# Batch 0 of a fused attention and MLP kernel: eleven idle matmuls ahead of k^T v, and v copied beside a column of ones

## The chip, the cores and the metric

The kernel runs on one core of one Trainium2 chip. The metric is the device time of one execution, in microseconds (us). Four executions of the kernel before gave 299.22, 299.75, 300.38 and 301.85 us, with a median of 300.06 us. The profile is that of one of them, the execution that took 299.22 us.

## The reference

Two stages follow each other. The first is a linear attention with cosine weights, for 8 batches, 8 heads, 576 positions and 64 columns a head:

```python
def phi(x, c, s):
    r = np.maximum(x, 0.0)
    return np.concatenate([r * c, r * s], axis=-1)
q_p = phi(q, cos_w, sin_w)          # 128 features a head
k_p = phi(k, cos_w, sin_w)
kv = np.einsum('bhsf,bhsd->bhfd', k_p, v)
z = np.sum(k_p, axis=2)
num = np.einsum('bhsf,bhfd->bhsd', q_p, kv)
den = np.einsum('bhsf,bhf->bhs', q_p, z)[..., None] + 1e-06
return (num / den).astype(np.float32)
```

The second is an MLP over the 4608 rows of 512 columns that come out: `h = x @ w_in` (512 by 2048), `g = h * sigmoid(1.702 h)`, `out = g @ w_out` (2048 by 512). The inputs and the output are float32.

## The kernel before

The order of instructions on each engine is written out by hand (a manual schedule); the tile framework adds the waits. The rows of x are cut into 9 blocks of 512. For each block, 16 tiles of `mm1` (L281, then gelu at L286) and four tiles of `mm2` (L321) run on TensorE, and the attention of the next batch is laid between them in pieces. Four PSUM banks serve in turn as `mm` tiles, and two pairs of banks as `at` tiles.

Nothing can cover the attention of batch 0: it is the start of the program, and the first MLP block needs it. Its order is written out ahead of the block loop. All its parts work on four heads (n = 0 or 1) or on two of four row chunks (p = 0 or 1).

- `warmup(12)` (L75): twelve matmuls on a zeroed tile, then two more ahead of each but the first transposing step.
- `prep_q0` and `turn_q0` (L364, L365): relu and cosine weights on q, transposes on TensorE, and copies to `qT` on ScalarE. Each of the four `turn_q0` takes one `mm` bank.
- `prep(0, "k", ...)` (L207 on VectorE, L205 on ScalarE): the features `kp` of k. There are 24 operations of 96 partitions by 4 heads by 64 columns: 18 of them on VectorE, and 6 (the sine weights of chunks 3 to 5) on ScalarE.
- `kv0` (L373, L375): k^T v of heads 0 to 3 in one `mm` bank, then of heads 4 and 5 and, after `num0(0, 0)`, of heads 6 and 7 in another. Each head takes six matmuls that accumulate over chunks of 96 rows. z is needed too, so each moving operand is a pattern over two 64-column pieces of the `v` tile: the piece of this head and chunk, and a piece at the tile's end that holds ones. 65 of the 128 columns that come out are copied to `kvs` by ScalarE.
- `num0` (L382): the numerator with the denominator as 65th column, for two row chunks and four heads.
- `den0` and `product0` (L394, L400, L401): on VectorE, the denominator plus 1e-6, its reciprocal, and the product, which gives `xb`.
- `turn_x0` (L409, L411): transposes of `xb` on TensorE into the rest of the numerator's own bank, and ScalarE's copy to `xT`.
- `mm1_first` (L417): `mm1` for the first four tiles of block 0, in column pieces as `xT` becomes available.

The `vt` tile, 66 columns for each chunk and head with ones in column 64 (L163), is used by the batches after the first: `prep_v_wide` (L210) copies batch 1's v there in one operation, `prep_v` (L213) those of the others, and `kv_half` (L244) multiplies with 65 columns.

GpSimd issues the loads in a fixed order (k and v of batch 0 in pieces, then w_in, w_out and the next batches); SP issues q of batch 0 and later the transposing DMAs.

Of the kernel before, what the change touches and what calls it, by code (L numbers as in the profile page):

```python
# [10 lines left out]
BF16 = mybir.dt.bfloat16  # L11
# [10 lines left out]
def kernel(  # L22
# [9 lines left out]
    nc = tc.nc  # L32
    B, H, S, D = q.shape
# [11 lines left out]
    two = ctx.enter_context(tc.tile_pool(name="two", bufs=2))  # L45
# [8 lines left out]
    def rows(c):  # L54
        return 128 if c < 4 else 64

    def wide(b, n):
        return b < 2 and n != "q"

    def krows(b, c):  # L60
        return 96 if b < 2 else rows(c)

    warm = const.tile([128, TB], BF16)
    nc.vector.memset(warm, 0.0)

    def mm_tile():
        return ps.tile([128, TB], F32, name="mm", bufs=4)

    def at_tile():
        return ps.tile([128, 2, 512], F32, name="at", bufs=2)  # L70

    def warmup(n):
        wps = at_tile()
        for _ in range(n):
            nc.tensor.matmul(wps[:, 0], warm[:, 0:128], warm, start=True, stop=True)  # L75


    state = {b: {} for b in range(B)}
    SRC = {"q": q, "k": k, "v": v}

    def load_main(b, n, h0=0, h1=H, on=nc.gpsimd):
        t = 6 if wide(b, n) else 4
        np_ = 96 if wide(b, n) else 128
        if h0 == 0:
            state[b][n] = two.tile([128, 2048 if n == "q" else 49 * D], BF16, name=n)
        on.dma_start(out=state[b][n][:np_, t * D * h0:t * D * h1].rearrange("p (h e) -> p h e", h=h1 - h0),  # L86
                     in_=SRC[n][b, h0:h1, 0:np_ * t, :].rearrange("h (p c) d -> p h (c d)", c=t))

# [9 lines left out]
    def load_all(b):  # L98
        for n in "qkv":
            load_main(b, n)  # L100
            load_tail(b, n)
# [21 lines left out]
    nc.gpsimd.iota(pos_i[:, 4:5], pattern=[[1, 1]], base=512, channel_multiplier=1)  # L123
    nc.gpsimd.iota(pos6_i, pattern=[[1, 6]], base=0, channel_multiplier=6)
    load_main(0, "k", 0, 4)
    nc.gpsimd.iota(id_i, pattern=[[1, 128]], base=0, channel_multiplier=-1)
    load_main(0, "k", 4, 8)
    load_main(0, "v", 0, 4)
    load_main(0, "v", 4, 6)
# [28 lines left out]
    kp = one.tile([128, 6, H, 2 * D], BF16, name="kp")  # L158
    vt = one.tile([128, 6, H, VW], BF16, name="vt")
    qT = one.tile([128, H, NC * 128], BF16, name="qT")  # L160
    qT_tail = one.tile([128, H, 128], BF16, name="qT_tail")
    nc.vector.memset(state[0]["v"][:, 48 * D:49 * D], 1.0)
    nc.vector.memset(vt[:, :, :, D:D + 1], 1.0)  # L163
    nc.vector.memset(qT[:, :, S:NC * 128], 0.0)
    nc.vector.memset(qT_tail[:, :, 64:128], 0.0)
# [16 lines left out]
    def part(b, n, c, h0, h1):  # L182
        if wide(b, n):
            return state[b][n][:96, 0:48 * D].rearrange("p (h c d) -> p c h d", c=6, d=D)[:, c, h0:h1]
        if c == 4:
            return state[b][n, 4].rearrange("p (h d) -> p h d", d=D)[:, h0:h1]
        return state[b][n][:, 0:32 * D].rearrange("p (h c d) -> p c h d", c=4, d=D)[:, c, h0:h1]
# [7 lines left out]
    def qn_slot(b, c):  # L195

        return state[b]["qn4"] if b < 2 and c == 4 else state[b]["qn"][:rows(c), c]

    def prep(b, n, c, h0=0, h1=H, on=(nc.vector, nc.vector)):
        r = rows(c) if n == "q" else krows(b, c)  # L200
        for cs, w in enumerate((cos6, sin6) if wide(b, n) else (cosw, sinw)):
            o = qn_slot(b, c) if n == "q" else kp[:r, c]
            oc, i, wc = o[:, h0:h1, cs * D:cs * D + D], part(b, n, c, h0, h1), w[:r, c:c + 1]
            if on[cs] is nc.scalar:
                nc.scalar.activation(oc, i, AF.Relu, scale=wc)  # L205
            else:
                nc.vector.tensor_scalar(oc, i, 0.0, wc, op0=MAX, op1=MUL)  # L207
# [149 lines left out]
    s0 = state[0]  # L357
# [7 lines left out]
        copy(qT[:, 4 * n:4 * n + 4, ds(256 * p, 256)].rearrange("p h (s t) -> p h s t", s=2), t)  # L365

    def kv0(kv, h0, h1):

        v3 = s0["v"][:96].rearrange("p (j d) -> p j d", d=D)
        for h in range(h0, h1):  # L370
            for c in range(6):
                j = h * 6 + c
                nc.tensor.matmul(kv[:, ts(h % 4, 128)].rearrange("p (j d) -> p j d", j=2), kp[:96, c, h, :],  # L373
                                 v3[:, j:49:48 - j, :], start=(c == 0), stop=(c == 5))
        nc.scalar.copy(s0["kvs"][:, h0 // 4, h0 % 4:h0 % 4 + h1 - h0, 0:D + 1],  # L375
                       kv.rearrange("p (h e) -> p h e", e=128)[:, h0 % 4:h0 % 4 + h1 - h0, 0:D + 1])

    def num0(n, p):
        nm = at_tile()
# [40 lines left out]
    AC, VE = nc.scalar, nc.vector  # L420
    kvs_new(0)
    warmup(12)

    def prep_q0(n, p, on=(VE, VE)):
# [5 lines left out]
    for n, p in ((0, 0), (0, 1), (1, 0), (1, 1)):  # L430
        if n:
            prep_q0(n, p)
        turn_q0(n, p, AC.copy)
        if (n, p) != (1, 1):
            warmup(2)
    for n in range(2):
        for c in range(6):
            prep(0, "k", c, 4 * n, 4 * n + 4, on=(VE, AC if c > 2 else VE))
    kv_lo, kv_hi = mm_tile(), mm_tile()
    kv0(kv_lo, 0, 4)  # L440
    kv0(kv_hi, 4, 6)
    na0 = num0(0, 0)
    kv0(kv_hi, 6, 8)
    product0(na0, den0(na0), 0, 0)
    nb0 = num0(1, 0)
# [30 lines left out]
    for i in range(NBLK):  # L476
        work = {n: [] for n in range(32)}
        b = i + 1
# [85 lines left out]
```

## Time and profile before

| what | value |
|---|---|
| median of four runs | 300.06 us (299.22 to 301.85) |
| profiled execution | 299.22 us |
| its span, first to last instruction | 297.3 us |
| mean granted TensorE clock | 0.994 |
| TensorE busy | 284.4 us (96%) |
| VectorE busy | 106.4 us (36%) |
| ScalarE busy | 125.8 us (42%) |
| GpSimd busy | 95.2 us (32%) |
| k^T v of batch 0 (L373) | 48 matmuls, 219 ns each from start to end, 11.5 to 15.4 us |
| idle matmuls (L75) | 18, the last ones at 8.9 us |
| first block's first full `mm1` tile (L281) | starts at 25.3 us |

In the rows of the profile, PE is TensorE's matmul, PEld its weight load, DVE is VectorE, ACT ScalarE, POOL GpSimd and SP SyncE. A row gives the start and the duration in us, the engine, the line, the operation, output and input tiles, their shapes, and how many instructions of that kind are merged in it; in brackets stand the idle time of the engine ahead of it and what ended it. A matmul's duration is that from its start to its end; in a run of them the starts lie closer together than that, so a row of several says how many were issued in how long. The granted clock is the share of full speed that the throttle left to TensorE.

### The profile page before, as it was taken

The numbers are of one execution on the slowest core, as the hardware profiler recorded it, in microseconds if no ns is written. First come the engines' busy times: TensorE is split into PE (matmuls) and PEld (weight loads), VectorE is DVE, ScalarE is ACT, GpSimd is POOL, SyncE is SP. The second block draws the span as 40 slices with busy tenths as digits, with TensorE's granted clock in tenths as the row PEclk, the third lists the DMA queues.
The fourth block names the chain that finished last, engine by engine and source line by source line (L and its number), as shares of the span: only waits on it lengthen the run. The fifth ranks groups of instructions, "written<-read, shape, count | busy, mean of one in ns | idle before, by whom it ended". The sixth has DMA issues, their size and how long they took to land.

```text
span 297.3 us, 5089 instructions
## 1 busy us (share of the span) xinstructions
PE 284.4 (96%) x1940; PEld 147.2 (50%) x1974; DVE 106.4 (36%) x357; ACT 125.8 (42%) x215; POOL 95.2 (32%) x117
## 2 busy tenths in 40 slices
PE   8778999999899999999999999999999999999994
PEld 3565456545444554455445544554455444444443
DVE  5851454683480158114811482148214200000000
ACT  6836623663126512651165116511751167127411
POOL 8532340540259015800590159004501200120021
PEclk9979999999999999999999999999999999999999
DMA  7999999599999977995799879964902510011033
GB/s 185 189 204 199 202 199 192 164 117 173 145 215 178 180 118 138 183 191 100 138 184 180 117 134 193 188 107 111 198 4 60 120 43 1 35 71 37 0 70 71
DMA packets 87303, 39.65 MB, mean 133 GB/s; under 512 B 57136, under 2 KB 85040, under 8 KB 87280
## 3 DMA queue, kind: packets, MB, share of 16 engines
q0 software_dynamic: 40848, 27.01, 58.8%
q1 hardware_dynamic: 46272, 12.20, 24.3%
q8 instruction: 15, 0.25, 0.3%
q10 hardware_dynamic: 160, 0.13, 0.2%
q14 instruction: 8, 0.07, 0.1%
HBM read 36.70 MB, written 9.44 MB: 155 GB/s over the span
## 4 chain that ended last, share of the span: by engine, by line
PE 88%; ACT 4%; DMA 4%; DVE 2%; issue 1%; ACTq 0%; DVEq 0%
PE mm L281 39%; PE mm L321 37%; DMA qT<-qn 4%; PE at L265 3%; PE at L244 3%; PE at L75 2%; PE mm L417 1%; ACT qT L365 1%; PE mm L345 1%; ACT g L286 1%; PE mm L373 1%; DVE xb L273 1%; ACT qT L226 1%; ACT xT L411 0%; ACT kp L205 0%
## 5 line engine op out<-in xcount | busy, mean ns | idle before, releaser
L321 PE MATMUL mm<-w_out_sb,g 128*128 128x512 bf16 x543 | 126.4, 379 | 0.6
L281 PE MATMUL mm<-xT,w_in_sb 128*128 128x512 bf16 x547 | 122.7, 377 | 0.9
L333 POOL DMA_DIRECT2D out_dram<-ysb x54 | 50.6, 942 | 175.3 <-ACT ysb L331 173.9
L286 ACT ACTIVATE g<-mm 128x512 bf16<-128x512 f32 x144 | 85.6, 598 | 45.9 <-PE mm L281 44.9
L281 PEld LDWEIGHTS <-w_in_sb 128*128 128x128 bf16 x564 | 54.3, 98 | 64.1 <-issue 0.2
L321 PEld LDWEIGHTS <-g 128*128 128x128 bf16 x560 | 52.2, 98 | 56.9
L331 ACT COPY ysb<-mm 128x512 f32<-128x512 f32 x34 | 19.9, 585 | 98.8 <-PE mm L321 98.8
L248 DVE CAST kvs<-at 128x260 bf16<-128x260 f32 x14 | 5.4, 426 | 60.3 <-PE at L244 60.3
L273 DVE TENSOR_TENSOR xb<-at,inv 128x512 bf16<-128x512 f32 (+1 forms) x36 | 24.8, 689 | 1.2
L271 DVE TENSOR_SCALAR den<-at 128x8 f32<-128x8 f32 (+1 forms) x36 | 5.9, 164 | 44.9 <-PE at L265 44.9
L350 DVE COPY ysb<-mm 128x256 f32<-128x256 f32 x1 | 0.4, 424 | 59.4 <-PE mm L345 59.4
L265 PEld LDWEIGHTS <-qT 128*128 128x128 bf16 x272 | 12.9, 98 | 9.4 <-DMA qT<-qn 1.7
L207 DVE TENSOR_SCALAR qn<-q,cosw 128x512 bf16<-128x512 bf16 (+1 forms) x36 | 12.4, 349 | 11.1 <-DMA q<-in_q_dram 11.1
L265 PE MATMUL at<-kvs,qT 128*128 128x65 bf16 x272 | 14.3, 194 | 1.4 <-DMA qT<-qn 0.8
L207 DVE TENSOR_SCALAR qn<-q,sinw 128x512 bf16<-128x512 bf16 (+1 forms) x34 | 13.1, 385 | 0.0
L86 POOL DMA_DIRECT2D v<-in_v_dram x10 | 9.8, 988 | 4.1 <-DMA v<-in_v_dram 2.4
L244 PEld LDWEIGHTS <-kp 128*128 128x128 bf16 (+1 forms) x288 | 9.6, 97 | 1.7
L244 PE MATMUL at<-vt,kp 128*128 128x65 bf16 (+1 forms) x288 | 9.8, 193 | 0.0
L86 POOL DMA_DIRECT2D k<-in_k_dram x9 | 7.8, 864 | 3.9 <-ACT g L286 3.1
L207 DVE TENSOR_SCALAR kp<-k,cosw 128x512 bf16<-128x512 bf16 x24 | 8.4, 352 | 0.0
L75 PE MATMUL at<-warm 128*128 128x512 bf16 x18 | 7.1, 548 | 1.2 <-DVE eps L151 1.2
L207 DVE TENSOR_SCALAR kp<-k,sinw 128x512 bf16<-128x512 bf16 x24 | 8.1, 340 | 0.0
(75 smaller groups left out, 138.0 us busy)
## 6 DMA issues: line engine op xcount, KB each, us to landing
out_dram<-ysb POOLq DMA_DIRECT2D x38, 128.0 KB, 2.9
out_dram<-ysb POOLq DMA_DIRECT2D x16, 256.0 KB, 2.8
q<-in_q_dram POOLq DMA_DIRECT2D x7, 512.0 KB, 9.4
k<-in_k_dram POOLq DMA_DIRECT2D x6, 512.0 KB, 10.8
v<-in_v_dram POOLq DMA_DIRECT2D x6, 512.0 KB, 12.4
w_out_sb<-in_moe_w_out_dram POOLq DMA_DIRECT2D x4, 512.0 KB, 18.1
w_in_sb<-in_moe_w_in_dram POOLq DMA_DIRECT2D x3, 512.0 KB, 12.4
q<-in_q_dram SPq DMA_DIRECT2D x2, 512.0 KB, 4.2
```

The lines of the kernel that those rows point to most:

```text
L75: nc.tensor.matmul(wps[:, 0], warm[:, 0:128], warm, start=True, stop=True)
L86: on.dma_start(out=state[b][n][:np_, t * D * h0:t * D * h1].rearrange("p (h e) -> p h e", h=h1 - h0), in_=SRC[n][b, h0:h1, 0:np_ * t, :].r ...
L207: nc.vector.tensor_scalar(oc, i, 0.0, wc, op0=MAX, op1=MUL)
L244: nc.tensor.matmul(kv[:, ds(h % 4 * (D + 1), D + 1)], kp[:r, c, h, :], vt[:r, c, h, 0:D + 1], start=(c == 0), stop=(c == last))
L265: nc.tensor.matmul(nm[:, h // 4, ds(h % 4 * (D + 1), D + 1)], q_slot(b, c)[:, h, :], state[b]["kvs"][:, h // 4, h % 4, 0:D + 1], start=Tru ...
L271: nc.vector.tensor_scalar(den[:r], nm4[:, :, :, D], 1e-6, None, op0=ADD)
L273: nc.vector.tensor_tensor(state[b]["xb"][:r, c].rearrange("p (n h) d -> p n h d", n=2), nm4[:, :, :, 0:D], inv[:r].unsqueeze(3).to_broadca ...
L281: nc.tensor.matmul(hps[:, c0:c1], w_in_sb[:, kc, ds(fc * 128, 128)], xT[:, kc, ds(i * TB + c0, c1 - c0)], start=(kc == 0), stop=(kc == KC ...
L286: nc.scalar.activation(g, hps, AF.Gelu_apprx_sigmoid)
L321: nc.tensor.matmul(yps, gT[fc][:, ds(t * 128, 128)], w_out_sb[:, fc, :], start=(fc == 0), stop=(fc == FC - 1))
L331: nc.scalar.copy(ysb, cur[t])
L333: nc.gpsimd.dma_start(out=out[row:row + (n - 1) * step + 1:step, :], in_=ysb[p0:p0 + n, :])
```

## The change

Three things change, all of them in batch 0's attention.

1. `warmup` can write to a given tile, and eleven more idle matmuls of 512 columns are issued between the last `turn_q0` and `kv0`. They take an `mm` tile of their own, so the tiles after it move on by one bank.
2. `kv0` begins with a copy on VectorE of its heads' v into `vt`, beside the column of ones: one operation for heads 0 to 3, one for heads 4 and 5, one for heads 6 and 7. In VectorE's order the three stand one after the other, behind all of `prep` of k and ahead of the first `den0`.
3. The matmuls of `kv0` read 65 columns of `vt` instead of two pieces of 64 columns of `v`, and write 65 columns a head. The piece of ones at the end of the `v` tile and its memset (L162) are gone.

```diff
-    def warmup(n):
-        wps = at_tile()
+    def warmup(n, wps=None):
+        wps = at_tile()[:, 0] if wps is None else wps
         for _ in range(n):
-            nc.tensor.matmul(wps[:, 0], warm[:, 0:128], warm, start=True, stop=True)
+            nc.tensor.matmul(wps, warm[:, 0:128], warm, start=True, stop=True)
...
-            state[b][n] = two.tile([128, 2048 if n == "q" else 49 * D], BF16, name=n)
+            state[b][n] = two.tile([128, 2048 if n == "q" else 48 * D], BF16, name=n)
...
-    nc.vector.memset(state[0]["v"][:, 48 * D:49 * D], 1.0)
...
     def kv0(kv, h0, h1):
-
-        v3 = s0["v"][:96].rearrange("p (j d) -> p j d", d=D)
+        nc.vector.tensor_copy(vt[:96, :, h0:h1, 0:D], s0["v"][:96, 6 * D * h0:6 * D * h1]
+                              .rearrange("p (h c d) -> p c h d", c=6, d=D))
         for h in range(h0, h1):
             for c in range(6):
-                j = h * 6 + c
-                nc.tensor.matmul(kv[:, ts(h % 4, 128)].rearrange("p (j d) -> p j d", j=2), kp[:96, c, h, :],
-                                 v3[:, j:49:48 - j, :], start=(c == 0), stop=(c == 5))
+                nc.tensor.matmul(kv[:, ds(h % 4 * (D + 1), D + 1)], kp[:96, c, h, :], vt[:96, c, h, 0:D + 1],
+                                 start=(c == 0), stop=(c == 5))
         nc.scalar.copy(s0["kvs"][:, h0 // 4, h0 % 4:h0 % 4 + h1 - h0, 0:D + 1],
-                       kv.rearrange("p (h e) -> p h e", e=128)[:, h0 % 4:h0 % 4 + h1 - h0, 0:D + 1])
+                       kv[:, 0:4 * (D + 1)].rearrange("p (h e) -> p h e", h=4)[:, h0 % 4:h0 % 4 + h1 - h0])
...
             prep(0, "k", c, 4 * n, 4 * n + 4, on=(VE, AC if c > 2 else VE))
+    warmup(11, mm_tile())
     kv_lo, kv_hi = mm_tile(), mm_tile()
     kv0(kv_lo, 0, 4)
```

In the changed kernel, line numbers behind L162 are lower by one, and by two or more behind `kv0`; the copies of v are L367 and the matmuls of k^T v L371.

## Prediction

> **What bounds the kernel now.** I read the page first, then the clock by stage, then the order of work in the first 26 us.
>
> ```profile
> span 297.3 us, 5089 instructions
> PE 284.4 (96%) x1940; PEld 147.2 (50%) x1974; DVE 106.4 (36%) x357; ACT 125.8 (42%) x215; POOL 95.2 (32%) x117
> ...
> PEclk9979999999999999999999999999999999999999
> ```
>
> TensorE is busy for 96% of the span and no other engine comes near. So time is won only where TensorE stands idle or runs at a low clock, and a microsecond won early arrives at the end whole, unless a later wait takes it back (after 25 us the longest wait of a matmul is 0.85 us, for a DMA at 79.9 us). The one low digit of the clock is slice 2, 14.9 to 22.3 us, which is where batch 0 goes through attention. The windows show it closely (PE, PEld, DVE, ACT and POOL busy, then granted clock, DMA share, GB/s):
>
> ```profile
> 17.00:17.50 0.50, 0.00 (x0) 0.10 (x1) 0.43 (x3) 0.00 (x0) 0.00 (x0) 0.81 1.30 227
> 17.50:18.00 0.50, 0.23 (x3) 0.23 (x3) 0.21 (x1) 0.00 (x0) 0.00 (x0) 0.50 1.13 188
> ...
> 20.50:21.00 0.50, 0.50 (x10) 0.50 (x9) 0.00 (x0) 0.00 (x0) 0.00 (x0) 0.77 1.30 202
> ```
>
> A mean of 0.81 is 0.38 of a window at 0.50, so the clock falls at 17.31; 0.77 puts its return at 20.73. The low stretch is 3.42 us long. If the clock is decided in equal stretches, the two before it are 10.47 to 13.89 and 13.89 to 17.31:
>
> ```profile
> 10.47:13.89 3.42, 2.19 (x34) 1.92 (x35) 2.73 (x12) 3.29 (x8) 2.69 (x4) 1.00 1.28 202
> 13.89:17.31 3.42, 2.04 (x38) 1.78 (x36) 2.09 (x9) 1.19 (x4) 1.68 (x3) 1.00 1.25 210
> 17.31:20.73 3.42, 2.96 (x33) 2.96 (x33) 1.30 (x3) 1.01 (x3) 0.77 (x1) 0.50 1.37 197
> ```
>
> 2.19 us of TensorE kept the clock, 2.04 us lost it, 2.96 us brought it back. The line between is thin. Now the work itself:
>
> ```profile
> 9.30 0.61 PE L364 MATMUL mm<-ident,qn 128*128 128x128 bf16 x8
> 11.51 0.63 PE L373 MATMUL mm<-v,kp 96*128 96x128 bf16 x5 [1.60 <-ACT kp L205]
> 12.31 1.90 PE L373 MATMUL mm<-v,kp 96*128 96x128 bf16 x31 [0.17 <-ACT kp L205]
> 14.05 0.42 PE L382 MATMUL at<-kvs,qT 128*128 128x65 bf16 x8
> 14.57 0.83 PE L373 MATMUL mm<-v,kp 96*128 96x128 bf16 x12
> ...
> 17.77 0.37 PE L409 MATMUL at<-ident,xb 128*128 128x128 bf16 x2 [1.44 <-DVE xb L401]
> 17.93 0.64 PE L382 MATMUL at<-kvs,qT 128*128 128x65 bf16 x8
> 18.39 1.04 PE L417 MATMUL mm<-xT,w_in_sb 128*128 128x128 bf16 x8
> ```
>
> Up to 17.77 us this stage is a chain through ScalarE, TensorE and VectorE, with TensorE waiting; from 17.77 to about 21 us TensorE itself is the limit, at half clock.
>
> **The change, part by part.** *Eleven idle matmuls.* In a run of 512-column matmuls one starts every 0.216 us (L321 in the chain: 28 in 6.04). The transposes issue until about 9.76, and 11 x 0.216 = 2.38 us brings the last start-to-start to 12.14. The bank that they write is the first of the four and ScalarE has emptied it since about 8.3. They lie in the 1.60 us and 0.17 us in which TensorE waits for kp, and end before v's copy (below), so they cost nothing. Without the cover of that copy they would hold k^T v from 11.51 to 12.14, of which little counts, since its sixth matmul waits for ScalarE until 12.31. At the low clock (12 in 5.30 us at the start, 0.43 each) they would last until 14.5 and cost 0.7 us; the clock shown here is 1.00.
>
> *The copies of v.* Three copies on VectorE stand behind all 18 kp operations of that engine.
>
> ```profile
> 12.11 1.09 DVE L207 TENSOR_SCALAR kp<-k,cos 96x256 bf16<-96x256 bf16 x3
> ...
> 40.09 0.95 DVE L210 COPY vt<-v 96x3072 bf16<-96x3072 bf16 x1
> ```
>
> VectorE is free at 13.20. For the price I take L210 (0.947 us for 3072) and L213 (0.276 us for 512 elements): 0.262 ns an element and 0.14 us fixed. So 1536 elements take 0.545 us, and 768 take 0.34 us and start about 0.27 apart. The first copy ends at 13.75, the others near 14.0 and 14.3. Three kp operations in 1.09 us are 0.42 us over their usual 0.67 (0.27, then two spaced 0.20) while GpSimd issues w_out from 12.41 to 13.90; the first copy lies there too. Bounds for it: 0.545 and 0.965 us. I take 0.545, the row of the same operation. The pieces of v need no further wait: issued from 3.17, 0.67 apart, and landing in about 8.3 us, by the DMA view they are there at 11.4, 12.1 and 12.8.
>
> *65 columns.* L244 does the same shape at 0.030 us (40 in 1.21 in the chain); the 128-column form takes 0.056 (31 in 1.90, less one's 0.22 us). 48 x 0.026 = 1.25 us of TensorE, which pays for most of the late start.
>
> *The sum up to 17.77.* A result comes some 0.16 us after its last start, and I allow 0.03 to 0.05 us for each hand-over. Heads 0 to 3: 13.80 + 24 x 0.030 + 0.16 = 14.69; their kvs copy on ScalarE (0.38) is done at 15.08, where before it was done at 13.96. Heads 4 and 5 are through TensorE by 14.89; their kvs copy runs 15.10 to 15.37. Heads 6 and 7 write the same bank and wait for that copy, as before: 15.42 + 0.36 + 0.16 = 15.94. The last kvs copy then starts at 15.96, where it was:
>
> ```profile
> 15.44 0.28 ACT kvs L375
> 15.76 0.36 PE at L382 x6
> 16.15 0.17 DVE den L394
> ```
>
> So that copy is 0.52 late, and `den` can start at 16.65. Behind the copies on VectorE stands the product of na0: num0(0, 0) at 15.12 to 15.38, den at 15.55, its product over at 16.67. Both arrive together: 16.65 against 16.15, and the turns of L409 start at 18.27 instead of 17.77. **Loss 0.5 us**, 0.9 us with the slow copy.
>
> *The clock after 17.77.* In the chain the low-clock pieces are 0.37 + 0.44 + 0.85 + 0.21 + 1.47 = 3.34 us, to 21.11. At full clock the same work is bound by ScalarE's two xT copies (0.37 each): turn 0.11, result 0.16, copy and hand-overs 0.45, so L417 starts after 0.72; then 8 x 0.056, 0.11 of turns, again 0.61 to the second copy's end (8 more matmuls lie beside it), and 8 x 0.056: 2.34 us. **Gain 1.0 us** if the clock stays. What follows (num0(1, 1), its product, the last turn) has the same lengths and was at full clock already.
>
> Does it stay? In 13.89 to 17.31 there are now 64 - 3 matmuls of 65 columns and 4 turns, 61 x 0.031 + 4 x 0.056 = 2.1 us of pure issue, where the old stretch had 3 + 12 of 128 columns, 16 of 65 and 4 turns, 15 x 0.056 + 16 x 0.032 + 4 x 0.056 = 1.6 us. That is clearly fuller. In 10.47 to 13.89 there are the idle matmuls (1.67) and the first three of k^T v (0.09): 1.76, against 36 - 3 = 33 x 0.056 = 1.85 before. So by issue the new first stretch lies between the one that kept the clock (1.85) and the one that lost it (1.6), nearer the keeper. I take it that the clock is kept.
>
> *The rest.* The memset of v (0.11 us at 2.80) ran ahead of 0.93 us of idle VectorE: nothing. SP's and GpSimd's queues hold the same instructions in the same order. The bank rotation moves by one, and the banks of k^T v are again the third and fourth of `first`: nothing.
>
> **Sum:** 0.5 - 1.0 = -0.5 us on a span of 297.3. The profiled execution took 299.22 us, the lowest of the four; their median is 300.06. I put the same difference on the median: **299.6 us**. A measurement of this kernel tells about 1% from no change, 3 us, and this is a sixth of it.
>
> The Trainium skill, "TensorE: Matmul & The Clock Gate", "Why this matters for your kernels", asks only that gaps between bursts stay under about 3 us. By it the clock would not have fallen in this trace, where the waits are 1.60 and 1.44 us; the rows show 0.50 all the same, and the rows decide. By the page alone the idle matmuls save nothing and the sum is +0.5. The same page, Part 1, says that the deciding window is 4096 cycles at 1.2 GHz (3.41 us; the trace shows 3.42) and runs free of the kernel's start. If so, where its edges fall changes from run to run, which no row here shows, and speaks against counting on eleven matmuls placed by one trace.
>
> **Rivals.** *The first stretch loses the clock (slower).* By the profile's busy time, which counts a matmul's tail, 10.47 to 13.89 holds 1.84 + 0.06 = 1.9 us, less than the 2.04 us that lost the clock. TensorE is idle from 12.3 to 13.8 for v's copy. If that decides, the clock falls at 13.89: k^T v at 0.055 a matmul adds 0.025 x 24 = 0.6 to heads 0 to 3 and 0.3 to heads 6 and 7, and with num0 and the tails about 1.15 us. Then the turns start at 19.4 and TensorE is nearly idle from 17.7 on, so the next stretch is thin too and the clock may fall again at 20.73, in the stage that gained (1.0 us back). +0.65 to +1.9 us, by the middle +1.5: 301.5. It decides from about 2.04 us of busy time downwards. Against it: the count by issue above.
>
> *The clock falls at 17.31 anyway.* For it: TensorE is still idle from about 17 to 18.27, waiting for `xb`. The turns then start 0.5 late into a low stretch that ends at 20.73, and 2.46 instead of 2.96 us run in it: 0.17 less loss. +0.33: 300.4. Against: the fuller stretch.
>
> *The idle matmuls do nothing because v's copy is slow.* With 0.965 us the loss is 0.9 and the gain still 1.0: -0.1, 300.0, or more if the later start empties the first stretch further, which is the first rival.
>
> **How the numbers follow.** Forecast (clock kept): 0.43, own range 298.7 to 300.4. First rival: 0.23 within 1% and 0.06 beyond it (two low stretches together with the slow copy, on runs that spread by 2.6 us themselves). Clock falls as before: 0.16. Slow copy with the clock kept: 0.09. The last 0.03 are for faster by over 1%, for which I find no place: nothing in this stage is worth 3 us. That makes 0.03 faster, 0.43 + 0.23 + 0.16 + 0.09 = 0.91 within 1%, 0.06 slower. The range reaches from the forecast with a gain of 1.5 us (the 1.0 with no late start and the rest for the spread of the runs) to a little beyond the first rival's middle: 298.4 to 301.7.
>
> **What would show it.** Right: clock 1.00 in every window from 10 to 25 us, first k^T v matmul near 13.8, three copies at L367 of about 0.55, 0.34 and 0.34 us, turns near 18.3 and the last 256-column group of the first four tiles starting near 23.7 instead of 24.20. Wrong: a clock of 0.50 anywhere between 13.9 and 24, a first copy near 1 us, or a start of k^T v after 14.2.

## The result, and the profile after

The changed kernel takes 298.28 us (median of 37 executions, 296.94 to 300.63), the kernel before 300.42 us (median of 58, 298.44 to 304.6). The ratio is 0.9929 with a 95% interval of 0.9912 to 0.9946, so the change brings 2.1 us, 0.7%. The forecast was a gain of 0.5 us and 299.6 us; the time lies 0.1 us under the range's lower end. Ratios and mean clocks leave out executions that are over 1.5% slower than the fastest of their kernel; the medians of the experiments do not.

The profiled execution of the changed kernel took 299.12 us, so it is slower than the median. The page:

```profile
span 297.1 us, 5103 instructions
PE 286.1 (96%) x1950; PEld 147.7 (50%) x1985; DVE 106.7 (36%) x359; ACT 126.1 (42%) x215; POOL 96.1 (32%) x117
...
PEclk9959999999999999999999999999999999999999
```

The clock has a lower digit in slice 2 (5) than before (7), and the span is only 0.2 us shorter. The windows show why; first the edges of the low part, then four stretches (PE, PEld, DVE, ACT and POOL busy, then granted clock, DMA share, GB/s):

```profile
15.50:16.00 0.50, 0.21 (x8) 0.11 (x5) 0.47 (x2) 0.27 (x1) 0.47 (x2) 0.94 1.23 205
22.50:23.00 0.50, 0.50 (x9) 0.50 (x8) 0.47 (x2) 0.39 (x1) 0.50 (x1) 0.73 1.25 207
...
9.10:12.50 3.40, 3.12 (x19) 1.39 (x18) 3.40 (x18) 3.36 (x7) 1.98 (x3) 1.00 1.27 194
12.50:15.94 3.44, 2.10 (x58) 1.92 (x59) 2.03 (x9) 1.74 (x6) 3.41 (x5) 1.00 1.23 203
15.94:19.35 3.41, 2.33 (x26) 2.00 (x26) 1.99 (x8) 1.22 (x3) 0.75 (x1) 0.50 1.25 207
19.35:22.73 3.38, 3.38 (x39) 3.38 (x37) 1.29 (x5) 0.49 (x2) 1.86 (x3) 0.50 1.38 199
```

The mean of 0.94 puts the fall at 15.94, that of 0.73 the return at 22.73: two low stretches, not none. The stretch with the idle matmuls (3.12 us busy) kept the clock; the one behind it, with k^T v (2.10 us), lost it. And the edges lie elsewhere than in the profile before, where a stretch ended at 17.31. The timeline of TensorE in the same execution:

```profile
9.73 2.54 PE L75 MATMUL mm<-warm 128*128 128x512 bf16 x10
13.47 1.26 PE L371 MATMUL mm<-vt,kp 96*128 96x65 bf16 x36 [1.20 <-DVE vt L367]
...
18.12 0.37 PE L407 MATMUL at<-ident,xb 128*128 128x128 bf16 x2 [1.04 <-DVE xb L399]
...
25.18 1.03 PE L415 MATMUL mm<-xT,w_in_sb 128*128 128x256 bf16 x8 [0.67 <-ACT xT L409]
...
79.88 0.42 PE L264 MATMUL at<-kvs,qT 128*128 128x65 bf16 x8
```

k^T v starts at 13.47 after a wait for v's copy, and the turns at 18.12. With two low stretches, the last 256-column group starts at 25.18, 0.98 us later than before (24.20). Yet the span is shorter. The last line tells where that was made good: in the kernel before, the same numerator of batch 2 waited for a transposing DMA:

```profile
79.92 0.43 PE L265 MATMUL at<-kvs,qT 128*128 128x65 bf16 x8 [0.85 <-DMA qT<-qn]
```

The changed kernel has no wait there. The first `mm1` tile of the next block starts at 87.30 us after the change and at 87.42 before; from there both need 209.8 to 209.9 us to the end of the span. So two places decide: batch 0's attention, and a wait near 80 us.

The clock of all executions says how typical a profile is. One stretch of 3.42 us at half clock lowers the mean of a 297 us span by 0.5 x 3.42 / 297 = 0.0058. The kernel before has means of 0.9845 to 0.9857 in the four sets of runs below, 2.5 to 2.7 stretches; its one profiled execution, at 0.994, had one, and none of the 101 executions in those sets had fewer (one of twelve in a repeat further down had, at 0.997). The changed kernel's mean is 0.9954 in the first measurement (0.8 stretches), and 15 of the 38 executions whose clock is listed were at 1.00, with a median of 297.64 us.

Seven more of them were at 0.997 to 0.999, less than one whole stretch. The mean also counts a low piece at the very end of the span, which costs nothing, since TensorE has no matmul left. The three profiles with such a mean have no other low piece. In the one at 0.998 (the second repeat below) the last matmul ends at 291.7 us and the clock falls at 294.12:

```profile
291.00:292.00 1.00, 0.70 (x7) 0.38 (x4) 0.21 (x1) 0.00 (x0) 0.00 (x0) 1.00 0.86 198
...
294.00:294.50 0.50, 0.00 (x0) 0.00 (x0) 0.00 (x0) 0.00 (x0) 0.00 (x0) 0.62 0.03 6
```

So 22 of the 38 executions kept the clock through batch 0. Without the end pieces the counts of stretches are 2.4 to 2.6 for the kernel before and 0.7 to 0.9 for the changed one.

### The profile page after: what moved, and what is told of

Its sections match the earlier page's. It is cut to its first block, busy times and chain, and to the rows that moved or that the text cites. A ratio compares the mean times of both kernels' runs of the same rounds, so it can differ in the third digit from the quotient of the medians.

```text
span 297.1 us, 5103 instructions
## 1 busy us (share of the span) xinstructions
PE 286.1 (96%) x1950; PEld 147.7 (50%) x1985; DVE 106.7 (36%) x359; ACT 126.1 (42%) x215; POOL 96.1 (32%) x117
## 4 chain that ended last, share of the span: by engine, by line
PE 89%; DVE 5%; ACT 2%; DMA 1%; issue 1%; ACTq 0%; DVEq 0%
PE mm L280 39%; PE mm L320 39%; PE at L264 3%; PE at L243 3%; PE mm L415 2%; DVE qn L206 2%; DMA q<-in_q_dram 1%; DVE kp L206 1%; PE mm L344 1%; ACT g L285 1%; DVE xb L272 1%; ACT qT L225 1%; PE at L380 1%; PE mm L371 0%; ACT xT L409 0%
## 5 line engine op out<-in xcount | busy, mean ns | idle before, releaser
L206 DVE TENSOR_SCALAR qn<-q,cosw 128x512 bf16<-128x512 bf16 (+1 forms) x36 | 12.6, 355 | 10.9 <-DMA q<-in_q_dram 10.9
## 6 DMA issues: line engine op xcount, KB each, us to landing
k<-in_k_dram POOLq DMA_DIRECT2D x6, 512.0 KB, 10.9
```

## The experiments

Two theories were to be told apart. By the first, the gain is batch 0's clock: the idle matmuls remove more low stretches than the one that the profile before showed, at about 1 us each. By the second, much of it is the wait for batch 2's transposed q near 80 us. Each run was timed beside the kernel before in the same set (medians 301.06, 301.3, 302.04 and 301.43 us).

### The parts alone

*Idle matmuls alone.* The kernel before with

```diff
+    warmup(11, mm_tile())
     kv_lo, kv_hi = mm_tile(), mm_tile()
```

and nothing else of the change.

> Only the eleven idle matmuls are added to the kernel before; k^T v stays in 128 columns and reads v itself. Theory 1 (the gain is TensorE's clock: each stretch of 3.4 us at half clock costs about 0.9 us, and the idle matmuls take such stretches away): at least 1.5 us below the kernel before, near 298.3 us or lower, since k^T v does not even start late; more executions at clock 1.00 than of the kernel before. Rival (the gain is the shorter k^T v of 65 columns, which also moves the work of later stages against their transfers): within 0.5 us of the kernel before, 300.4.

Measured: 299.07 us, ratio 0.9921 (0.9887 to 0.9955), mean clock 0.9970. The eleven matmuls alone bring the whole gain, since the changed kernel in the same set stands at the same ratio (below). The wait near 80 us is there in its profile, and longer than before:

```profile
80.61 0.43 PE L265 MATMUL at<-kvs,qT 128*128 128x65 bf16 x8 [1.55 <-DMA qT<-qn]
```

So the second theory can't be the whole of it.

*Copy and 65 columns alone.* The changed kernel without the idle matmuls:

```diff
-    warmup(11, mm_tile())
```

> The changed kernel without the eleven idle matmuls: v is copied, k^T v has 65 columns. Theory 1 (clock): no gain; k^T v starts at 13.5 us behind an empty stretch of TensorE of some 3.5 us, the clock falls at least as often as before, 300.4 to 301.5 us. Rival (65 columns): most of the gain is here, 298.3 to 299 us.

Measured: 304.3 us, ratio 1.0116 (1.0075 to 1.0158), slower than before by 3.2 us and slower than either theory had said, with all clocks between 0.976 and 0.982. Its windows, and further down those from 84 us:

```profile
9.90:13.33 3.43, 0.00 (x0) 0.00 (x0) 3.43 (x16) 3.27 (x7) 2.34 (x4) 1.00 1.25 194
13.33:16.74 3.41, 3.04 (x54) 3.02 (x55) 1.21 (x5) 0.65 (x2) 2.80 (x3) 0.50 1.24 206
16.74:20.15 3.41, 1.93 (x28) 1.65 (x26) 2.13 (x8) 1.05 (x3) 0.77 (x1) 0.50 1.33 201
20.15:23.50 3.35, 3.35 (x40) 3.35 (x38) 0.90 (x2) 0.82 (x3) 1.51 (x2) 0.50 1.29 204
...
84.00:86.00 2.00, 0.94 (x10) 0.68 (x11) 0.25 (x2) 0.00 (x0) 0.01 (x1) 0.75 1.14 236
86.00:88.00 2.00, 2.00 (x6) 0.65 (x5) 0.81 (x2) 0.00 (x0) 0.00 (x0) 0.50 0.89 250
```

With no idle matmuls TensorE has nothing at all from 9.90 to 13.33 (a wait of 4.06 us for v's copy), and three low stretches follow. The timeline shows the rest:

```profile
13.70 2.16 PE L371 MATMUL mm<-vt,kp 96*128 96x65 bf16 x36 [4.06 <-DVE vt L367]
...
79.84 0.43 PE L264 MATMUL at<-kvs,qT 128*128 128x65 bf16 x8 [0.50 <-DMA qT<-qn]
...
85.06 0.62 PE L264 MATMUL at<-kvs,qT 128*128 128x65 bf16 x8 [3.06 <-DMA qT<-qn]
```

3.56 us are lost to the transposed q, and another low stretch follows that wait (0.50 in 86 to 88).

*The changed kernel again*, unchanged, in the same set.

> The changed kernel again, beside the other three on one chip, to have executions with their clocks: both theories 298.3 us. Theory 1: executions at clock 1.00 at 297.6 us, with one low stretch (0.994) 0.9 us more, with two (0.989) 1.8 us more.

Measured: 299.07 us, ratio 0.9924 (0.9889 to 0.9959), mean clock 0.9941. At clock 1.00 its executions take 297.31 to 297.97 us, at 0.994 they take 298.24 to 300.46.

*Eighteen idle matmuls* instead of eleven (`warmup(18, mm_tile())`), to fill the wait for v's copy.

> The changed kernel with eighteen idle matmuls in place of eleven: they last 18 x 0.216 = 3.9 us, to 13.65 us, and so close the wait of 1.2 us for v's copy but start k^T v about 0.2 us late. Theory 1 (clock): fewer executions with a low stretch, median 0.2 to 0.7 us below the changed kernel, 297.6 to 298.1. Rival (65 columns): 0.2 us above the changed kernel, 298.5.

Measured: 299.42 us, ratio 0.9961 (0.9932 to 0.9991), mean clock 0.9975. The clock is a little better than with eleven and the time is not, against both theories. The profile is that of the slowest of the twelve executions (302.65 us), so it can't speak for the median. In it k^T v starts at 13.50, no later than with eleven, but a numerator at 79.8 us waits 2.22 us, and the clock is low from 79.7 to 83.2. The version with seventeen (below) has such a wait, of 1.80 us, in an ordinary execution.

*Narrow idle matmuls.* The changed kernel with eleven matmuls of 64 columns:

```diff
-    warmup(11, mm_tile())
+    small = mm_tile()
+    for _ in range(11):
+        nc.tensor.matmul(small[:, 0:64], warm[:, 0:128], warm[:, 0:64], start=True, stop=True)
```

> The changed kernel with eleven idle matmuls of 64 columns in place of 512: the same number of instructions in the same place, but 11 x 0.03 = 0.3 us of TensorE in place of 2.4. Theory A, if it is TensorE's busy time that keeps the clock: as without idle matmuls (copy only), 303 to 304.5 us at a mean clock near 0.978. Rival (any instruction in the gap keeps it): 299 us as the changed kernel.

Measured: 300.03 us, ratio 0.9948 (0.9923 to 0.9973), mean clock 0.9834. The number of instructions is that of the changed kernel, and the clock is lost all the same:

```profile
9.24:12.66 3.42, 0.98 (x20) 0.77 (x18) 3.42 (x18) 3.38 (x7) 1.99 (x3) 1.00 1.25 185
12.66:16.07 3.41, 2.59 (x46) 2.57 (x47) 1.30 (x6) 1.33 (x4) 3.38 (x5) 0.50 1.20 198
```

0.98 us of work in the stretch ahead of k^T v did not keep the clock; 3.12 us did. So it is the width of the idle matmuls that counts and not their number; the bank order is that of the changed kernel too. The time was a miss of 3 to 4 us against the expectation, and the profiled execution has no wait near 80 us:

```profile
80.75 0.42 PE L264 MATMUL at<-kvs,qT 128*128 128x65 bf16 x8
```

Its batch 0 ends within 0.4 us of that of the copy alone (first full `mm1` tile at 27.11 and 27.52), and the one waits 3.56 us and the other not at all.

### The wait near 80 us

*Later loads.* The aim was to issue the next batch's loads later, so that the transposes would not queue behind them:

```diff
-                at(1, load_all, b + 1)
+                at(9 if i == 1 else 1, load_all, b + 1)
```

in the kernel before, in the changed one, and in the one with both gaps filled (below).

> The kernel before, with the loads of batch 3 issued in step 9 of block 1 in place of step 1, so that the transposing transfers of batch 2's q (58 to 74 us) do not share the transfer engines with them. Theory A (the kernel before loses to half clock in batch 0's attention, up to 26 us): still 1.5 us or more above the changed kernel with the same edit (next run), 300 us or more. Theory B (most of it is lost at 76 to 85 us, where TensorE waits for those transposing transfers, 0.85 us in the profile of before, and the clock can fall once more): near 298.5 us, within 0.6 us of the next run.

> The changed kernel with the same edit. Theory A: 298.5 to 299 us, the gap of 1.5 to 2 us to the run before it stays. Theory B: 298.2 us, and the gap shrinks to 0.6 us or less.

> Both edits on the changed kernel: filled waits and late loads of batch 3. Theory A: 297.4 us, as the run before it. Theory B: 297.3 us too, but 1 us or more below the run before it, with hardly any spread.

The edit does nothing: GpSimd's queue holds the same instructions in the same order, behind the same stores, so the loads go out at the same time (batch 3's q at 57.15 us in the second of the three, at 56.93 us in the changed kernel of the last set below). The three runs are repeats of the kernels that they start from: 301.52 us (ratio 0.9985, 0.9945 to 1.0024), 298.28 us (0.9914, 0.988 to 0.9947) and 299.11 us (0.996, 0.9924 to 0.9996). As repeats they are of use. The first shows an ordinary execution of the kernel before, at a clock of 0.977:

```profile
7.78:11.20 3.42, 1.71 (x19) 1.00 (x17) 3.42 (x16) 3.20 (x5) 1.32 (x2) 1.00 1.25 180
11.20:14.60 3.40, 2.66 (x26) 2.69 (x27) 1.67 (x8) 1.87 (x5) 2.41 (x4) 0.50 1.25 200
14.60:18.00 3.40, 3.24 (x35) 3.11 (x34) 1.06 (x3) 0.88 (x3) 1.67 (x2) 0.50 1.24 208
...
21.40:24.80 3.40, 3.40 (x38) 3.40 (x37) 1.31 (x5) 0.44 (x2) 1.50 (x2) 0.50 1.25 206
```

Here the clock falls at 11.20, ahead of k^T v (11.94), and comes back at 24.85 only: four low stretches where the profile before had one. The first full tile starts at 28.36 instead of 25.26, 3.1 us later for three stretches more. The second repeat shows the changed kernel with the clock kept, used below.

*Both gaps filled.* The changed kernel with idle matmuls up to v's copy, and five more in the wait for `xb`:

```diff
-    warmup(11, mm_tile())
+    warmup(17, mm_tile())
...
+    first = [mm_tile() for _ in range(4)]
+    warmup(5, first[0])
```

> The changed kernel with 17 idle matmuls in place of 11 and 5 more ahead of the turns of nb0, so that both waits of TensorE in batch 0's attention (12.3 to 13.4 and about 17 to 18.1 us) are filled without starting anything later. Theory A: no low stretch up to 26 us, first full tile of block 0 at 24.4 us in place of 26.2, nearly all executions at clock 1.00 and 297.4 us. Theory B: the same clock up to 26 us, but the wait for batch 2's q stays and the median is 298.5 or more.

Measured: 299.37 us, ratio 0.9949 (0.9912 to 0.9985), mean clock 0.9987. Full clock in nearly every execution, and still no gain over the changed kernel (0.9914 in the same set). The profile, at full clock, shows where it goes:

```profile
24.66 3.61 PE L280 MATMUL mm<-xT,w_in_sb 128*128 128x512 bf16 x15
...
80.27 0.43 PE L264 MATMUL at<-kvs,qT 128*128 128x65 bf16 x8 [1.80 <-DMA qT<-qn]
```

The first full tile starts within 0.02 us of that in the second repeat above (24.64), which has no wait; the first transposes of batch 2's q are issued at 58.17 and 58.15 us. So the time at which batch 0 ends is not what decides the wait.

*Later numerators.* What waits can be moved instead: the numerators of batch 2 stand later in block 1.

```diff
+            if i == 1:
+                ks = (17, 19, 21, 25, 27)
```

This was put into the kernel before, the changed one, and the one with both gaps filled.

> The late loads changed nothing, because GpSimd's queue does not follow TensorE's steps and held the same instructions; those runs were the kernel before and the changed kernel once more. This is another way to take the wait for batch 2's q away: the kernel before, with the numerators of batch 2's chunks 3 and 4 two steps later in block 1 (25 and 27 in place of 23 and 25), so that TensorE works for 1.7 us more before it needs the transfer. Theory A (half clock in batch 0's attention): 300 to 301 us, still 1.5 us or more above the next run. Theory B (the wait at about 80 us): 299 us or less, within 0.6 us of the next run.

> The changed kernel with the same edit. Theory A: 298 to 298.5 us, 1.5 us or more below the run before it; what the wait still cost here (up to 0.5 us of the median) is gone. Theory B: the same as without the edit, and as the run before it.

> Both waits in batch 0's attention filled (17 and 5 idle matmuls) and the late numerators: full clock, 24.65 us at the first full tile, and no wait at 80 us. Theory A: 297.4 us with little spread, below the changed kernel and the run before it. Theory B: also 297.4; but then the kernel before with late numerators is not above 298.5.

Measured: 300.06 us (ratio 0.9916, 0.9887 to 0.9945), 298.56 us (0.9879, 0.9844 to 0.9914) and 298.03 us (0.9868, 0.9836 to 0.9901). None of the three profiles has the wait. The kernel before gains 0.8% by the move alone. The version with both gaps filled, at a mean clock of 0.9992, is the fastest that was run; the changed kernel itself measured 0.9893 (0.9853 to 0.9933) in the next set, so the two can't be told apart.

*Later still* (`ks = (17, 19, 21, 27, 29)`), in the kernel before, the changed one and the copy alone, beside the changed kernel itself.

> The kernel before with the numerators of batch 2's chunks 3 and 4 four steps later (27 and 29), which leaves 3.4 us more for the transfer of q: no wait at 80 us even at the 3.06 us that copy only had. If batch 0's attention makes 1.5 of the 2.1 us and the wait the rest: 300 us, 1.5 us above the next run. If the wait makes most of it: 299 us or less, within 0.6 us of the next run.

> The changed kernel with the same edit. By the first reading 298.2 to 298.6 us, 1.5 us below the run before it; by the second 298.3 and equal to it.

> Copy only (no idle matmuls ahead of k^T v) with the same edit. If its 304.3 us came from the wait at 80 us and the low stretch behind it (3.6 us of wait in its profile), on top of a first full tile at 27.5 us: 300.5 to 301 us, and never below the run with the kernel before. If they came from batch 0's attention alone: 304 us still.

> The changed kernel as it is, for the gap with and without the later numerators on one chip: 298.3 to 299 us, 2 us below the kernel before, and equal to the run of it with later numerators within 0.4 us, because its profiles show no wait at 80 us.

Measured:

| kernel | us | ratio (interval) | mean clock |
|---|---|---|---|
| before, later numerators | 299.72 | 0.9959 (0.9928 to 0.9990) | 0.9842 |
| copy alone, later numerators | 300.15 | 0.9949 (0.9917 to 0.9981) | 0.9828 |
| changed, later numerators | 298.75 | 0.9896 (0.9857 to 0.9936) | 0.9920 |
| changed | 298.63 | 0.9893 (0.9853 to 0.9933) | 0.9940 |

The move is worth 0.4% on the kernel before and nothing on the changed one. The copy alone goes from 304.3 to 300.15 us, a little under what was expected of it: most of its loss was the wait and the low stretch behind it, not the copy. Without the wait, the 1.0 us that is left between before and changed goes with the clock: by the means 1.3 stretches fewer, less the late start of some 0.4 us (next section). In the kernel before with later numerators the median is 298.43 us at a clock of 0.994, 299.76 at 0.989 and 301.4 at 0.976: three stretches for 3.0 us, 1.0 us each.

The listed executions show the wait at an equal clock too. At 0.989, the kernel before took 300.02 to 302.41 us in this set (nine executions, median 300.59), and with later numerators 299.60 to 299.83 (three, median 299.76). This fits a wait that differs from execution to execution in the kernel before and is worth 0.8 us there.

**Both theories hold in part.** Batch 0 makes the quotient of the ratios without the wait: 0.9879 / 0.9916 = 0.996 and 0.9896 / 0.9959 = 0.994, or 1.1 and 1.9 us; the medians give 1.5 and 1.0. The whole difference of the plain kernels was 2.1 us in the first measurement and 2.8 in the last set, which leaves 0.2 to 1.7 us for the wait; the move alone, on the kernel before, gave 1.2 and 2.5 us by its ratios. About 1 us is a fair reading. The intervals are some 1 us wide to each side; a finer split isn't to be had from these runs.

## Why the prediction was right or wrong

The second repeat of the changed kernel kept the clock (295.6 us of span), and so shows the forecast's own case:

```profile
13.68 1.26 PE L371 MATMUL mm<-vt,kp 96*128 96x65 bf16 x36 [1.40 <-DVE vt L367]
...
18.20 0.27 PE L407 MATMUL at<-ident,xb 128*128 128x128 bf16 x2 [1.12 <-DVE xb L399]
...
23.58 1.03 PE L415 MATMUL mm<-xT,w_in_sb 128*128 128x256 bf16 x8 [0.67 <-ACT xT L409]
24.64 1.67 PE L280 MATMUL mm<-xT,w_in_sb 128*128 128x512 bf16 x6
```

- *Idle matmuls at no cost: right.* k^T v waits for v's copy, not for them: 1.40 us here, 1.20 in the profile after. (The 0.43 us of the low clock was read from the first twelve matmuls, where the windows give 1.00; the spacing at 0.50 is the same, 8 in 3.34 us from 85.49 in the copy alone.)
- *The copies: right.* The group of line 367 in the profile after (shortest, middle and longest, in ns) agrees with 0.34, 0.34 and 0.545 us. In the second repeat the longest took 775 ns, inside the two bounds given.

```profile
L367 DVE COPY vt<-v x3: 347/349/548, 12.9 to 13.6; 96x768 bf16<-96x768 bf16 x2, 96x1536 bf16<-96x1536 bf16 x1
```

- *65 columns: right.* 36 starts in about 1.1 us, 0.030 each.
- *The sum up to the turns: right.* Forecast 18.27, measured 18.20; the loss is 0.43 us against 17.77, where 0.5 was said.
- *A low stretch costs 1.0 us: right.* The last 256-column group starts at 23.58 (forecast 23.7, before 24.20), which is 0.6 us earlier in spite of a start 0.4 us later, and the executions sorted by clock give 1.0 us a stretch.
- *"Does it stay? ... I take it that the clock is kept": half wrong.* It is kept in 22 of 38 executions. In the other 16 it is lost, and the profile after shows the sign that was named as wrong. The comparison of stretches was made for edges at 10.47, 13.89 and 17.31, and other executions have other edges: falls at 15.94, 11.20 and 13.33 in the profiles above. In the profile after, idle matmuls and k^T v were split so that k^T v's stretch held only 2.10 us. The line between 2.04 and 2.19 us did not hold either: other executions kept the clock with 1.84 and 1.87 us (last section).
- *"Gain 1.0 us if the clock stays", the 1.0 in the sum: the step that failed.* It prices one low stretch. It was mis-sized by taking the one profiled execution of the kernel before as its usual one. The prediction saw that this execution was the lowest of the four, and still put its difference on the median. By the mean clocks the kernel before loses 2.5 to 2.7 stretches and the changed one 0.8 to 1.0, so the term is 1.5 to 1.9 stretches, not one. With the late start of 0.5 that is a gain of 1.0 to 1.4 us instead of 0.5.
- *"The longest wait of a matmul is 0.85 us, for a DMA at 79.9 us": read, and given no price, the other step that failed.* The prediction used it only as a thing that might take gains back, and the opposite happened: none of the changed kernel's four profiles shows it. It was the second term that was missing, of about 1 us. That the changed kernel would lose the wait could not be read from the profile before, and why it does stays open.
- *The rivals.* The clock falling in the first or second stretch was a rival in both forms, and something like it happens in 16 of the 38 executions. Both were priced as if the kernel before always had one stretch, so they came out as loss or near nothing. The 0.7% lies within the 1% that the likeliest cases were given, but for reasons that none of them had.

The warning taken from the Trainium skill ("TensorE: Matmul & The Clock Gate", Part 1, that the window runs free of the kernel's start) was the best hint, and it was used against the change alone. The same sentence holds for the kernel before, and there it says that one profile is a single draw. The runs here agree with it in the edges named above. By the same page's gap rule of about 3 us ("Why this matters for your kernels"), only the copy alone, with 4.06 us of idle TensorE, and the narrow idle matmuls, with 3.26 us, would lose their clock; the kernel before loses it with waits of 1.60 and 1.44 us, so a shorter gap does not protect the clock in this case.

**Open:** what decides the wait near 80 us. The transposes of batch 2's q take some 10 to 11 us from issue to landing while loads share the DMA engines (median of five: 10.9 us before, 10.1 after), so they have little to spare. But runs whose first transposes are issued within 0.02 us of each other differ in it by 1.8 us, and it can't be said from these runs why the four profiles of the plain changed kernel show none and those of its variants do. Its other executions may have it: at a clock of 0.994 they took 298.24 to 300.46 us in one set. Only its removal was tried with success; the attempt at the loads changed nothing.

## What to carry to other kernels

Read the granted clock of every execution that is listed, not only that of the profiled one, and price a clock effect by the mean number of low stretches, without those behind the last matmul. Where TensorE must wait for a chain on other engines, full-width idle matmuls of 2 to 3 us in that wait are worth having; the same number of narrow ones did not keep the clock here. Any wait for a DMA further on is a term of the sum, with both signs, also where the change is far away from it: look at what stands there, and move the waiting work a few steps later if it has the room.

## What the runs showed of the hardware

- The clock is not decided by the length of the longest gap: it was lost in the profile after, whose waits ahead of the fall are 1.20 us and less, and kept in the second repeat with one of 1.40 us. In stretches of 3.4 us at full clock, it was lost with 0.00, 0.98, 1.71, 2.04 and 2.10 us of busy TensorE and kept with 2.19 and 3.12. Busy time alone does not settle it either: the clock was kept with 1.87 us (8.04 to 11.45, the kernel before with later numerators) and 1.84 us (7.89 to 11.31, the copy alone with those still later). At half clock, 2.96 us busy brought it back in the profile before, and 2.71 us in the copy alone with later numerators (18.13 to 21.55), but 3.24 us did not in the stretch from 14.60 of the repeat.
- The clock in the rows does not cover the start: the twelve first matmuls of 512 columns are 0.43 us apart with 1.00 in the rows (1.20 to 6.50 us of the profile before), where such matmuls are 0.216 us apart later.
- The number of low stretches in the same program goes from one (0.994) to four (0.977) in the profiles of the kernel before and from none (0.998) to two (0.986) in those of the changed one. This is a large part of the spread of its times, but not all: at an equal 0.989 the kernel before took 299.58 to 302.63 us in the four sets.
- A wait for a DMA of 3.06 us at 85 us, in the middle of a program whose TensorE is 94% busy, was followed by a low stretch of its own; one of 1.80 us at 80 us was not.
